# A two-layer SSM-convolution and GeGLU kernel: the last down add of a visit, ahead of or behind the next feature tile's gelu and product

## The chip, the cores and the metric

The kernel runs on one core of a Trainium2 chip. The metric is the device time of one execution in microseconds (us); lower is better. The engines are named as the profile names them: PE (TensorE, matmuls; PEld is its weight loads), DVE (VectorE), ACT (ScalarE), POOL (GpSimd) and SP (SyncE, which here issues DMAs). Each engine runs its own list of instructions in order and waits on semaphores for the others.

## The reference

Two layers of the same pair of steps over a sequence of 2048 positions with 576 channels, batch 1. Step A is a gated long convolution, step B a GeGLU feed-forward with 4608 features. Both normalise their input.

```python
def _A_ref(q, k, v, shift_k, ssm_k, ssm_D):
    ...                       # k_shift: causal filter of 4 taps over k
    kv = k_shift * v
    ...                       # y: causal convolution of kv with ssm_k (2048 taps a channel) by FFT
    y = y + kv * ssm_D[None, None, :]
    return q * y

def _B_ref(x, w_gate, w_up, w_down):
    return (_gelu(x @ w_gate) * (x @ w_up)) @ w_down

x = A_q
x = x + _A_ref(_layernorm(x, axis=-1), A_k, A_v, A_shift_k, A_ssm_k, A_ssm_D)
x = x + _B_ref(_layernorm(x, axis=-1), B_w_gate, B_w_up, B_w_down)
x = x + _A_ref(_layernorm(x, axis=-1), A_k, A_v, A_shift_k, A_ssm_k, A_ssm_D)
x = x + _B_ref(_layernorm(x, axis=-1), B_w_gate, B_w_up, B_w_down)
return x
```

Inputs, weights and output are bf16. The convolution part depends on k, v and the filters alone, so both layers share its result; only the gate q differs.

## The kernel before

The sequence is cut into four chunks of 512 rows (`CH`), and a chunk into four row quarters of 128 (`RT`, index `j`). A *unit* is one layer of one chunk; there are eight. The convolution is done chunk by chunk by a blocked transform made of small matmuls (`cps` tiles, lines 288 and 331) with products and sums on DVE.

The feed-forward sets the frame. Its 4608 features are 36 tiles of 128, in three phases of 12 (`FP`). The units are taken in passes, `[[0], [1, 2], [3, 4], [5, 6], [7]]`; within a pass, each phase is done for each of its units, so that a weight tile serves two units. One phase of one unit is a *visit* (the loop at line 1354); there are 24, counted from 0. A visit has two parts:

- Twelve feature tiles (line 1387). For each, `gu` (line 889) issues 18 matmuls that make gate and up, 128 features by 512 rows each, in one PSUM tile; then ACT makes `ga` = gelu(gate) and DVE makes `hT` = `ga` times up (lines 1410 and 1411; in the early visits, while `hurry()` holds, lines 1401 to 1403 copy `up` out by ACT as well).
- Four row quarters (`j`). For each, 24 down matmuls (line 1426) make `dn`, 128 rows by 576 channels, in a PSUM tile, and DVE adds it to the running `x_c`.

The add has several forms. In the first phase it is line 1466 (it also takes off a mean that an earlier step left in), in the second line 1468, in the third line 1460 for layer 0 (it also sums the row, for the next normalisation). These three are made by `plus` and put into the queue `late` with the planner's time at which the matmuls will be done. In layer 1's third phase the add (line 1447) writes the output tile and is issued at once, without `late`.

PSUM has four such tiles. One is the convolution's (`cps`); the other three are handed out in turn by `pr`, to `gu`, `dn` and, between downs, to further `cps`. A tile is free for its next matmuls once whatever reads it is done: `hT` for a `gu`, the add for a `dn`. `pr` counts what it hands out in `taken` and puts out a late add at the latest when its tile is about to come round again.

The order of instructions on every engine is fixed while the program is built. There is no scheduler behind it (`manual_schedule`); a small clock model, `Pace`, keeps an estimated time for PE (`t.pe`), DVE and ACT, and greedy steps use it. `fill(limit, ...)` (line 941) is called after every feature tile and after every down step. It issues due loads, then late adds (`run_late`, line 624: the first in the queue if its time has come and DVE would be done by `limit`), then convolution steps and normalisation steps for DVE as far as they fit, then ACT steps, then convolution matmuls. Weight loads (`load_wgu`, `load_wd`) and the transposes that make a unit's `xnT` (`spread`, line 841) all go out on SP's queue; rows that are late are turned on PE instead (`turn_row`, line 897).

For a feature tile the order of recording is: `gu`, then gelu and `hT`, then `fill`. At the first tile of a visit the add of the previous visit's fourth row quarter is as a rule still in `late`, since the last down step is not followed by a `fill`. `run_late` reads

```python
if not late or late[0][0] > t.pe or max(t.dve, t.pe - 1.0) + C_EVD > limit:
    return False
```

and `NEVER` is 1e9.

Of the kernel before, what the change touches and what calls it, by code (L numbers as in the profile page):

```python
# [27 lines left out]
NEVER = 1e9  # L28
# [553 lines left out]
def ssm_geglu_kernel(ctx, tc, A_q, A_k, A_v, A_shift_k, A_ssm_k, A_ssm_D, B_x, B_w_gate, B_w_up,  # L582
# [41 lines left out]
    def run_late(limit):  # L624
        if not late or late[0][0] > t.pe or max(t.dve, t.pe - 1.0) + C_EVD > limit:
            return False
        ready, _, run = late.popleft()
        run()
        t.on_dve(C_EVD, ready)
        return True  # L630

    def pr(name):
        while late and taken[0] - late[0][1] >= 2:
            ready, _, run = late.popleft()
            run()
            t.on_dve(C_EVD, ready)
        taken[0] += 1
        return bank(turn[(taken[0] - 1) % 3], name)
# [247 lines left out]
    def gu(pair, w, gi, cols, xnT):  # L886
        for k in range(NKC):
            for s, r0 in ((0, 0), (1, HK)):
                nc.tensor.matmul(cols(pair[:, s, :]), lhsT=w[r0:r0 + HK, k, gi * P:(gi + 1) * P],  # L889
                                 rhs=cols(xnT[r0:r0 + HK, blk_of[k], :]), start=(k == 0), stop=(k == NKC - 1))  # L890

    def gu_half(pair, fi, n):
        gu(pair, wgu[fi // FG], fi % FG, lambda a: a.rearrange("p (j q) -> p j q", q=P)[:, n::2, :], xnT_of[0])
# [27 lines left out]
    def when_due(when, load, n):  # L921
        due.append((when, len(due), load, n))
        due.sort(key=lambda d: d[0])
# [17 lines left out]
    def fill(limit, tensor, conv_first):  # L941
        weights()
        conv.run_loads()
        spreads(tensor=tensor)
        while True:
            if run_late(limit):
                continue
            if conv_first:
                if not (conv.run_v(limit) or run_vq(limit)):
                    break  # L950
            elif not (run_vq(limit) or not pressing() and conv.run_v(limit)):
                break
        run_aq(min(limit, t.pe + 2.3))
        if tensor:
            for _ in range(3):
                if pressing() and (units[coming[0]][1], RT - 1) in conv.y_at or not conv.run_p():
                    break
# [10 lines left out]
    with tc.manual_schedule():  # L968
# [385 lines left out]
        for at, (wb, ph, ui, first, final) in enumerate(visits):  # L1354
# [32 lines left out]
            for fi in range(FP):  # L1387
                n, gi = divmod(wb * FP + fi, FG)
                w = wgu[n]
                if wb == 0 and fi in early:  # L1390
                    pair = early.pop(fi)
                    taken[0] += 1
                    gu_half(pair, fi, 1)
                    t.pe = max(t.pe, free.popleft()) + C_GU / 2
                else:
                    pair = pr("gu")
                    gu(pair, w, gi, lambda a: a, xnT)
                    t.pe = max(t.pe, free.popleft()) + C_GU
                if hurry() and t.act <= t.pe + 0.2:
                    ga = work.tile([P, 2, CH], BF16, tag="ga", name="ga")  # L1400
                    nc.scalar.activation(out=ga[:, 0, :], in_=pair[:, 0, :], func=ACT.Gelu_apprx_tanh)  # L1401
                    nc.scalar.copy(out=ga[:, 1, :], in_=pair[:, 1, :])  # L1402
                    nc.vector.tensor_tensor(out=hT[:, fi, :], in0=ga[:, 0, :], in1=ga[:, 1, :], op=ALU.mult)  # L1403
                    there = t.on_act(2 * C_GELU, max(t.pe + 0.15, gone[0]))
                    gone.append(t.on_dve(C_HB, there + 0.15) + 0.1)
                    free.append(there + 0.1)
                    lead = FAR
                else:
                    ga = work.tile([P, CH], F32, tag="ga", name="ga")
                    nc.scalar.activation(out=ga[:], in_=pair[:, 0, :], func=ACT.Gelu_apprx_tanh)  # L1410
                    nc.vector.tensor_tensor(out=hT[:, fi, :], in0=ga[:], in1=pair[:, 1, :], op=ALU.mult)  # L1411
                    gone.append(t.on_dve(C_HT, t.on_act(C_GELU, max(t.pe + 0.15, gone[0])) + 0.15) + 0.1)
                    free.append(gone[-1])
                    lead = LEAD
                if gi == FG - 1 and final:
                    when_due(t.pe + (FP - FG) * C_GU + 12.0, load_wgu, n + 3)
                fill(t.pe + C_GU + lead, hurry(), conv.left > 0)
# [57 lines left out]
@with_exitstack  # L1475
def kernel(
    ctx: ExitStack,
    tc: tile.TileContext,
    A_q: bass.AP,
    A_k: bass.AP,  # L1480
    A_v: bass.AP,
    A_shift_k: bass.AP,
    A_ssm_k: bass.AP,
    A_ssm_D: bass.AP,
    B_x: bass.AP,
    B_w_gate: bass.AP,
    B_w_up: bass.AP,
    B_w_down: bass.AP,
    out: bass.AP,
):  # L1490
    ssm_geglu_kernel(tc, A_q, A_k, A_v, A_shift_k, A_ssm_k, A_ssm_D, B_x, B_w_gate, B_w_up,
                     B_w_down, out)
# [30 lines left out]
```

## Time and profile before

| | us |
|---|---|
| median of 3 runs | 954.97 (954.17 to 955.44) |
| profiled execution, its own time | 954.88 |
| profiled execution, span from the first to the last instruction | 953.1 |
| granted PE clock, mean (1 is full) | 1.000 |

Where the profile's page groups instructions by line, the rows that the change is about are these:

| line, engine, what | count | mean ns |
|---|---|---|
| L889 PE `gu` matmul, 512 columns | 5130 | 376 |
| L1426 PE `dn` matmul, 288 columns | 2304 | 286 |
| L1410 ACT gelu | 256 | 597 |
| L1411 DVE `hT` | 256 | 686 |
| L1466 DVE add, first phase | 28 (and 4 of the first unit) | 815 |
| L1468 DVE add, second phase | 32 | 751 |
| L1460 DVE add, third phase of layer 0 | 16 | 755 |
| L1447 DVE add to the output tile | 15 | 753 |

Busy times of pipelined matmuls overlap, so 376 ns is not the distance between two of them: ten tiles of 18 `gu` matmuls take 19.60 us in the chain of waits, 1.96 a tile. Ends of matmuls are modelled; starts are recorded.

How to read it: the page gives busy shares of the engines and the chain of work that ended last. A wait is named with the engine and line that ended it. "Stretches" are windows in time, with the busy time of each engine in them.

### The profile page before, as it was taken

To read this page: it belongs to the slowest core of one execution; us is meant where nothing else is said; L and a number is where in the kernel's file an instruction comes from. 1 tells how busy PE (TensorE), PEld (TensorE's weight loads), DVE (VectorE), ACT (ScalarE), POOL (GpSimd) and SP (SyncE) were. 2 spreads that over 40 slices of the span, in tenths; PEclk is the share of its full clock that TensorE was granted. 3 is DMA by queue.
4 is the path that set the end of the run, shared out by engine and by line. 5 is a ranking of instruction groups with operands and counts; after the bars stand their busy time and mean duration, and the time that the engine had idled before them with its cause. 6 is when DMAs were issued, how large, how long until landed. Compare 5 with 4: busy or idle time off the path is not lost.

```text
span 953.1 us, 19333 instructions
## 1 busy us (share of the span) xinstructions
PE 933.3 (98%) x8225; PEld 536.5 (56%) x8225; DVE 550.0 (58%) x1034; ACT 326.2 (34%) x590; POOL 136.2 (14%) x302
## 2 busy tenths in 40 slices
PE   8899999999999999999999999999999999999998
PEld 5756456564655655556556556456456456456455
DVE  7776676586898866667887722553332333532322
ACT  5665426442324136441222511551211214411211
POOL 3214101221113004221110200130000002100000
PEclk9999999999999999999999999999999999999999
DMA  9998997348724803993771730591540540596630
GB/s 238 268 238 203 271 250 145 113 87 224 224 76 132 198 1 88 175 250 86 160 226 38 139 85 22 93 204 33 110 115 1 114 111 8 96 245 151 144 68 26
DMA packets 125323, 130.14 MB, mean 137 GB/s; under 512 B 39730, under 2 KB 117427, under 8 KB 125236
## 3 DMA queue, kind: packets, MB, share of 16 engines
q1 hardware_dynamic: 115906, 92.46, 45.3%
q0 software_dynamic: 9200, 35.54, 12.1%
q8 instruction: 64, 1.05, 0.5%
q10 hardware_dynamic: 130, 0.90, 0.3%
q14 instruction: 23, 0.19, 0.1%
HBM read 108.53 MB, written 11.80 MB: 126 GB/s over the span
## 4 chain that ended last, share of the span: by engine, by line
PE 87%; DVE 5%; DMA 5%; ACT 2%; issue 1%; SPq 0%; ACTq 0%; DVEq 0%
PE gu L889 55%; PE dn L1426 28%; DMA nat<-in_A_ssm_k_dram 2%; PE cps L288 2%; DVE hT L1411 1%; ACT ga L1410 1%; PE cps L331 1%; DMA wgu<-in_B_w_gate_dram 1%; DVE x_c L1466 1%; DMA Hd<-hh 1%; PE ps L889 1%; DMA k<-in_A_k_dram 1%; DVE x_c L1468 1%; PE ps L1092 0%; DVE x_c L1460 0%
## 5 line engine op out<-in xcount | busy, mean ns | idle before, releaser
L889 PE MATMUL gu<-xnT,wgu 64*128 64x512 bf16 x5130 | 562.1, 376 | 4.8 <-DVE x_c L1466 1.8
L889 PEld LDWEIGHTS <-wgu 64*128 64x128 bf16 x5238 | 251.8, 94 | 315.3 <-issue 8.2
L1411 DVE TENSOR_TENSOR hT<-ga,gu 128x512 bf16<-128x512 f32 x256 | 175.7, 686 | 252.8 <-ACT ga L1410 251.5
L1410 ACT ACTIVATE ga<-gu 128x512 f32<-128x512 f32 x256 | 152.8, 597 | 491.1 <-PE gu L889 485.1
L1426 PE MATMUL dn<-wd,hT 128*128 128x288 bf16 x2304 | 294.3, 286 | 0.5 <-DVE xn L1436 0.5
L1426 PEld LDWEIGHTS <-hT 128*128 128x128 bf16 x2304 | 223.5, 98 | 66.0 <-issue 10.5
L721 POOL TENSOR_SCALAR means<-s 128x1 f32<-128x1 f32 x28 | 11.2, 401 | 267.7 <-DVE x_c L1460 224.8
L1468 DVE TENSOR_TENSOR x_c<-x_c,dn 128x576 f32<-128x576 f32 x32 | 24.0, 751 | 32.3 <-PE dn L1426 32.3
L291 ACT ACTIVATE eo<-cps 128x576 f32<-128x576 f32 x48 | 30.9, 651 | 26.9 <-PE cps L288 14.9
L737 POOL TENSOR_TENSOR rstd<-ve,neghalf_t 128x1 f32<-128x1 f32 x56 | 34.4, 615 | 4.7
L308 DVE TENSOR_TENSOR prod<-prod 128x576 bf16<-128x576 bf16 x72 | 33.0, 458 | 2.5
L1466 DVE SCALAR_TENSOR_TENSOR x_c<-dn,means,x_c 128x576 f32<-128x576 f32 x28 | 22.8, 815 | 19.8 <-PE dn L1426 19.7
L1401 ACT ACTIVATE ga<-gu 128x512 bf16<-128x512 f32 x29 | 17.3, 597 | 44.5 <-PE gu L889 41.2
L397 POOL DMA_DIRECT2D kr<-Kd x24 | 13.1, 546 | 100.5 <-DVE prod L307 100.5
L401 POOL DMA_DIRECT2D hr<-Hd x36 | 19.4, 541 | 45.4 <-DVE prod L307 45.4
L1403 DVE TENSOR_TENSOR hT<-ga 128x512 bf16<-128x512 bf16 x31 | 13.0, 421 | 20.8 <-ACT ga L1402 20.8
L1447 DVE TENSOR_TENSOR xn<-x_c,dn 128x576 bf16<-128x576 f32 x15 | 11.3, 753 | 23.0 <-PE dn L1426 23.0
L729 ACT ACTIVATE junk<-x_c,nm 128x576 bf16<-128x576 f32 x28 | 21.5, 767 | 4.9 <-POOL nm L721 4.9
L1460 DVE SCALAR_TENSOR_TENSOR x_c<-dn,x_c 128x576 f32<-128x576 f32 x16 | 12.1, 755 | 18.1 <-PE dn L1426 17.8
L763 ACT ACTIVATE yh<-y,rstd 128x576 f32<-128x576 bf16 x28 | 21.4, 767 | 3.1 <-POOL rstd L737 2.3
L721 POOL TENSOR_SCALAR nm<-s 128x1 f32<-128x1 f32 x28 | 8.6, 308 | 90.0 <-DVE x_c L773 89.9
L296 DVE TENSOR_TENSOR kc<-eo 128x288 bf16<-128x288 f32 x48 | 19.3, 453 | 3.7 <-ACT eo L291 2.2
(148 smaller groups left out, 601.5 us busy)
## 6 DMA issues: line engine op xcount, KB each, us to landing
wgu<-in_B_w_gate_dram SPq DMA_DIRECT2D x45, 576.0 KB, 6.0
wd<-in_B_w_down_dram SPq DMA_DIRECT2D x30, 864.0 KB, 8.9
wgu<-in_B_w_up_dram SPq DMA_DIRECT2D x45, 512.0 KB, 8.0
hr<-Hd POOLq DMA_DIRECT2D x36, 288.0 KB, 6.1
kr<-Kd POOLq DMA_DIRECT2D x24, 288.0 KB, 5.9
Kd<-kc POOLq DMA_DIRECT2D x12, 288.0 KB, 3.8
Hd<-hh POOLq DMA_DIRECT2D x12, 288.0 KB, 3.9
k<-in_A_k_dram POOLq DMA_DIRECT2D x3, 1008.0 KB, 11.6
```

Of the source, the lines that this page charges most:

```text
L291: nc.scalar.activation(out=eo[:], in_=ps[:, :, 0:HW], func=ACT.Copy, scale=scale)
L308: nc.vector.tensor_tensor(out=dst, in0=pr[:, 0, :], in1=pr[:, 1, :], op=ALU.subtract if part == 0 else ALU.add)
L721: nc.gpsimd.tensor_scalar(out=v["nm"][:], in0=v["s"][:], scalar1=-1.0 / D, scalar2=None, op0=ALU.mult)
L729: nc.scalar.activation(out=junk[:], in_=get_x(), func=ACT.Square, bias=v["nm"][:, 0:1], accum_out=v["ss"][:])
L737: nc.gpsimd.tensor_tensor(out=v["rstd"][:], in0=ve[:], in1=neghalf_t[:, 0:1], op=ALU.pow)
L763: nc.scalar.activation(out=g["yh"][:], in_=conv.y[c][:, j, :], func=ACT.Identity, scale=g["rstd"][:, 0:1], bias=1.0)
L889: nc.tensor.matmul(cols(pair[:, s, :]), lhsT=w[r0:r0 + HK, k, gi * P:(gi + 1) * P], rhs=cols(xnT[r0:r0 + HK, blk_of[k], :]), start=(k == 0 ...
L1410: nc.scalar.activation(out=ga[:], in_=pair[:, 0, :], func=ACT.Gelu_apprx_tanh)
L1411: nc.vector.tensor_tensor(out=hT[:, fi, :], in0=ga[:], in1=pair[:, 1, :], op=ALU.mult)
L1426: nc.tensor.matmul(acc[:, h, 0:HW], lhsT=hT[:, fi, j * P:(j + 1) * P], rhs=wd[2 * wb + fi // WT][:, fi % WT, h * HW:(h + 1) * HW], start=( ...
L1466: nc.vector.scalar_tensor_tensor(out=xh, in0=acc[:, :, 0:HW], scalar=m_[:, 0:1], in1=xh, op0=op, op1=ALU.add)
L1468: nc.vector.tensor_tensor(out=xh, in0=xh, in1=acc[:, :, 0:HW], op=ALU.add)
```

## The change

Two lines are added in the loop over feature tiles, behind `gu` and ahead of the tile's gelu and product. They call `run_late` with no limit until the first add in the queue is not yet ready by the planner's clock or none is left.

```diff
                     pair = pr("gu")
                     gu(pair, w, gi, lambda a: a, xnT)
                     t.pe = max(t.pe, free.popleft()) + C_GU
+                while run_late(NEVER):
+                    pass
                 if hurry() and t.act <= t.pe + 0.2:
                     ga = work.tile([P, 2, CH], BF16, tag="ga", name="ga")
```

Lines below the place have numbers higher by two in the changed kernel: the adds of lines 1460, 1466 and 1468 become 1462, 1468 and 1470, the output add of 1447 becomes 1449, and `hT` of 1411 becomes 1413.

## The prediction

> **What bounds the kernel now.** I read the page's busy shares first, then the chain, then who waited for whom on the weight-load queue, then the stretches visit by visit, then one boundary instruction by instruction. A visit is one pass of the loop over `visits`: 12 feature tiles of gate/up matmuls (`gu`, 18 each) and then four row quarters of down matmuls (`dn`, 24 each). I count visits from 0; there are 24.
>
> The page:
>
> ```profile
> span 953.1 us, 19333 instructions
> PE 933.3 (98%) x8225; PEld 536.5 (56%) x8225; DVE 550.0 (58%) x1034; ACT 326.2 (34%) x590; POOL 136.2 (14%) x302
> ...
> PE 87%; DVE 5%; DMA 5%; ACT 2%; issue 1%; SPq 0%; ACTq 0%; DVEq 0%
> ```
>
> TensorE (PE) sets the end: 87% of the chain. The 5% of VectorE (DVE) and 2% of ScalarE (ACT) are places where PE stands still. The waits of PE's weight loads (waiter, releaser: us in total, times, longest) say where:
>
> ```profile
> PEld L889 <- DVE x_c L1466: 5.8, 8, 0.9
> PEld L889 <- DVE x_c L1468: 5.2, 8, 0.8
> ...
> PEld L889 <- DVE x_c L1460: 2.8, 4, 0.7
> ```
>
> L889 is `gu`; L1466, L1468 and L1460 are the three forms of the down add. 8 + 8 + 4 = 20 waits. There are 23 boundaries between visits, and three of them follow a visit of layer 1's last phase, whose add is L1447 and never enters `late`. So every boundary behind a late add has one wait, and no other has. One boundary in the chain, piece by piece (start, length, what):
>
> ```profile
> 734.95 0.73 PE dn L1426 x6
> 735.69 2.07 PE gu L889 x18
> ...
> 737.78 0.60 ACT ga L1410
> ...
> 738.40 0.69 DVE hT L1411
> 739.09 0.68 DVE x_c L1468
> ...
> 739.81 1.25 PE gu L889 x9
> ```
>
> The fourth down ends at 735.7, but its add starts at 739.0: it stands on DVE behind `hT` of feature tile 0, which needs gelu, which needs the whole of `gu` 0. The third feature tile takes the PSUM bank that the add reads, so its matmuls start at 739.81 instead of two tiles (2 x 1.96 us) after 735.62, at 739.54. DVE itself was idle for 4.87 us ahead of that `hT`.
>
> What a wait costs is read from the stretches between first `gu` starts (length, PE busy, ...):
>
> ```profile
> 735.62:771.21 35.59, 35.45 (x313) 19.66 (x313) 11.18 (x16) 7.16 (x12) 0.00 (x0) 1.00 0.52 102
> 806.80:842.47 35.67, 35.46 (x313) 19.67 (x313) 14.77 (x28) 11.62 (x22) 6.58 (x16) 1.00 0.69 121
> 842.47:877.75 35.28, 35.28 (x313) 19.74 (x312) 11.46 (x16) 7.16 (x12) 0.54 (x1) 1.00 0.78 182
> ```
>
> Same matmuls, same granted clock of 1.00. The last one follows an L1447 add, which starts at 842.58, right behind its down, and it takes 35.28 us. Behind L1468 a visit takes 35.59, behind L1466 or L1460 35.66 or 35.67. The kernel holds its own experiment: an add that is put out at once costs PE nothing.
>
> **The change part by part.** It adds no instruction. The new loop puts out every add that the planner's clock calls ready, after `gu` of a tile is recorded and before that tile's gelu and `hT`. In the order of the changed program (built, not run), the fourth add stands directly ahead of the next visit's first `hT` at all 20 boundaries, where it stood directly behind it before.
>
> *Removed: 20 waits.* Behind L1466: seven of 35.66 - 35.28 = 0.38, and the first (visit 1 takes 35.87) of 0.60, 3.26 in all. Behind L1468: seven of 0.31; visit 2 carries other work, its idle time there is 0.35 where the 0.31 ones show 0.14 and the 0.38 ones 0.20, so with the same 0.17 to 0.18 on top it is 0.53; 2.70 in all. Behind L1460: four of 0.38 to 0.39, 1.54. Sum 7.50 us. The add costs nothing in its new place: it takes 0.75 to 0.82 us from about 735.7, and the `hT` behind it can't start before gelu ends at 738.38, 1.9 us after the add. In loaded visits up to six convolution steps stand before the add, but there too DVE was idle before `hT` 0 (2.95 us at 135.3). Late next would be tile 3, which needs the bank of `hT` 0: `hT` 0 ends at 739.09, tile 3 is due at 741.5, 2.4 us of cover. Had the `hT`s to slip by the add's 0.75, 1.6 would be left.
>
> The idle column and the stretches differ. PE's waits for the three adds sum to 1.8 + 0.8 + 0.4 = 3.0 us, and seven of 0.14 that are too short for that list make it 4.0, not 7.5. The Trainium skill ("Perfetto Trace Analysis", section "Tensor Engine Instruction (MATMUL, LD_WEIGHTS)") states that a TensorE end time is estimated by the profiler and not observed; by the idle column the gain would be 4.0, by the starts 7.5. I go by the starts, since 35.59 against 35.28 is measured between starts alone.
>
> *Moved: the greedy planner's later choices.* As DVE's clock is charged earlier, visits 2 to 4, 6 to 8 and 12 come out with their matmuls in another order; that of the other 17 is unchanged. One move has a price. In visit 2 the last of the three rows turned on PE stands at the very end, so the next visit waits for its copy (start, length):
>
> ```profile
> 172.84 0.52 PE cps L905 x9
> ...
> 173.38 0.77 DVE xnT L910
> ...
> 174.19 2.13 PE gu L889 x18
> ```
>
> PE idles 0.85 us there, 1.02 between starts by the same 0.17. In the changed order four convolution and four down matmuls stand between, 8 x 0.124 = 0.99 us (a down phase is 11.87 us for 96), against a copy of 0.77 and two hops. I take 0.8 saved; bounds 1.0 saved and, if the row is not ready four down matmuls earlier, 0.5 lost.
>
> *Re-dealt: convolution tiles between downs.* Visits 3, 4, 7 and 8 take 40.10, 40.90, 44.64 and 40.56. Undisturbed they would take 35.28 plus 0.124 for each of 32 (in visit 7, 64) further matmuls: 39.24 and 43.19. Less the add's wait that leaves 0.48, 1.28, 1.14 and 0.93, together 3.8 us of waits for evacuations and crosses. Their new order has the same number of tiles at similar spacing; visit 8 gets exactly the spacing that visit 4 had. I take no change; bounds: all 3.8 gone, or doubled.
>
> *Queues.* SyncE: in visit 8 the third pair of transposes of visit 9's `xnT` now stands behind one weight load (three DMAs) instead of before it. Before, that load was issued at 389.8, the last pair at 396.4, landing by 406.0; the first reader starts at 411.64: 5.6 us of cover, so 0. GpSimd: small statistics and spills change places, and the mean behind L1460 starts some 3 us earlier; no wait of PE hangs on them at the boundaries. DMA issues are the same in number.
>
> *Sum.* 953.1 - 7.5 - 0.8 = 944.8 us of span. The profiled execution took 954.88, 1.8 over its span, and the median shown is 954.97, 0.1 from it. So 946.6.
>
> **The rivals.**
>
> *The adds go, but the re-dealt order gives part back.* For: DVE is 65 to 85% busy in visits 1 to 8, and 3.8 us already wait there. Against: no step is added. If these waits double, 950.4; with the turned row's saving gone too, 951.2. If only the idle column's 4.0 comes back, 946.6 + 3.5 = 950.1.
>
> *The change doesn't do what it says*: tile 2 waits for something else that is as late, say its weights or `hT` 0. Against: the 35.28 visits, and the 0.72 us between `hT` 0's end and tile 2's start, which is the add's length. About 955.
>
> *Slower: visit 9 starves for `xnT`.* One mechanism: two pairs of transposes behind a weight load on SyncE while the DMA engines are 94% busy (371 to 412). The slowest transpose took 13.6 us to land. A delay up to 5.6 us is free; from 5.6 + 8.3 = 13.9 it eats all that is gained. At 20 us it gives 955 + 6 = 961. For: SyncE stood for 44 us at 327 on one such pair with nothing issued behind it, and a load issued at 403 landed at 417. Against: the load waits for no buffer at that point (its group's last reader, visit 8's first four tiles, is done by 379), so it goes out before 389.8 rather than after, and the pair behind it loses at most the load's 6.5 us of issue.
>
> **How the numbers follow.** The forecast, 944 to 949, has 0.64. The part given back (949 to 953) has 0.18, no effect (within 0.2%, 953.1 to 956.9, what a measurement of this kernel can't tell from no change) 0.05, slower 0.08, and all waits of the convolution gone as well (below 943.5, down to 946.6 - 3.8 - 0.2 = 942.6) 0.05. Faster: 0.64 + 0.18 + 0.05 = 0.87. Range 943.5 to 951.2, the upper end being the doubled waits without the turned row: 0.64 and most of 0.18, about 0.8.
>
> **What would show it.** Right: L1466, L1468 and L1460 gone from the waits of L889; visits behind them 35.28 long; the add starting within 0.2 us of its down's end in the last third; PE's share of the chain up and DVE's near 2 to 3%. The turned row: no 0.85 us of idle at the start of visit 3. Wrong would be: tile 2 still starting late with another releaser; tile 3 waiting for `hT` 0; visits 3, 4, 7, 8 longer than 40 to 45 us by more than they give; or PE waiting for `xnT` at the start of visit 9.

## The result, and the profile after

The changed kernel takes 947.87 us (median of 7 runs, 947.52 to 953.15) against 954.97 before (954.17 to 960.04): ratio 0.9923, 95% interval 0.9897 to 0.9949. The forecast was 946.6, range 943.5 to 951.2. The profiled execution has a span of 946.1, against 953.1 before and 944.8 in the forecast's sum. Some executions of either kernel take 4 to 6 us longer than the rest, which widens these ranges.

The page of the changed kernel, busy shares and chain:

```profile
span 946.1 us, 19330 instructions
PE 930.2 (98%) x8225; PEld 539.2 (57%) x8225; DVE 552.5 (58%) x1033; ACT 327.5 (35%) x591; POOL 137.5 (15%) x302
...
PE 96%; DVE 2%; DMA 1%; ACT 1%; issue 0%; POOL 0%; SPq 0%; ACTq 0%; DVEq 0%
```

Busy times hardly move: nothing became cheaper. DVE's part of the chain falls from 5% to 2%, and PE's rises from 87% to 96%. (Part of that rise is in the first 90 us, where the chain runs through DMAs before and through PE now, although visit 1 starts at 96.2 in both.)

Who PE waited for, in the changed kernel (us in total, times, longest):

```profile
PE cps L288 <- DVE x_c L1468: 2.0, 3, 0.7
PE cps L288 <- ACT eo L291: 1.3, 3, 0.7
...
PE gu L889 <- DMA xnT<-xn: 0.6, 1, 0.6
PE dn L1428 <- DVE xn L1438: 0.5, 1, 0.5
```

No `gu` (L889) waits for an add any more. One `gu` wait is new: for a DMA that makes `xnT`. The waits of `cps` tiles between downs are still there.

A boundary that answers to the one at 735.6, in the timeline (start, length, engine, line, what, idle time before):

```profile
730.30 4.92 PE L889 MATMUL gu<-xnT,wgu 64*128 64x512 bf16 x44
730.41 0.76 DVE L1470 TENSOR_TENSOR x_c<-x_c,dn 128x576 f32<-128x576 f32 x1 [2.19 <-PE dn L1428]
732.46 0.60 ACT L1412 ACTIVATE ga<-gu 128x512 f32<-128x512 f32 x1 [13.32 <-PE gu L889]
733.09 0.69 DVE L1413 TENSOR_TENSOR hT<-ga,gu 128x512 bf16<-128x512 f32 x1 [1.93 <-ACT ga L1412]
```

The add starts 0.11 us after the visit's first `gu` matmul, instead of 3.4 us after it. `hT` still waits for gelu, 1.93 us after the add has ended, and `gu` runs on without a break. The stretches from first `gu` to first `gu` (length, PE busy, ...), two behind a late add and one behind an output add, then visits 2 and 3:

```profile
553.89:589.17 35.28, 35.28 (x313) 19.76 (x314) 11.28 (x16) 7.16 (x12) 1.70 (x3) 1.00 0.19 63
730.30:765.59 35.29, 35.29 (x314) 19.78 (x314) 11.28 (x16) 7.16 (x12) 0.00 (x0) 1.00 0.52 102
836.15:871.44 35.29, 35.29 (x315) 19.77 (x314) 11.47 (x16) 7.16 (x12) 0.54 (x1) 1.00 0.72 169
131.47:173.16 41.69, 41.69 (x376) 24.47 (x376) 28.76 (x65) 23.02 (x43) 7.14 (x18) 1.00 0.82 175
173.16:214.29 41.13, 39.21 (x341) 24.16 (x341) 26.88 (x55) 19.90 (x38) 12.30 (x30) 1.00 0.49 132
```

The visits 1 to 22 that hold no convolution matmuls are now all 35.28 or 35.29 long. From visit 9 on the saving is 4.2 us, as in the forecast's sum for those visits. The miss is in visits 2 to 8: 2 and 3 together took 82.26 before and take 82.82, although two add waits worth 0.91 left them.

### The profile page after: what moved, and what is told of

Its sections match the earlier page's. It is cut to its first block, busy times and chain, and to the rows that moved or that the text cites. A ratio compares the mean times of both kernels' runs of the same rounds, so it can differ in the third digit from the quotient of the medians.

```text
span 946.1 us, 19330 instructions
## 1 busy us (share of the span) xinstructions
PE 930.2 (98%) x8225; PEld 539.2 (57%) x8225; DVE 552.5 (58%) x1033; ACT 327.5 (35%) x591; POOL 137.5 (15%) x302
## 4 chain that ended last, share of the span: by engine, by line
PE 96%; DVE 2%; DMA 1%; ACT 1%; issue 0%; POOL 0%; SPq 0%; ACTq 0%; DVEq 0%
PE gu L889 59%; PE dn L1428 29%; PE cps L288 2%; PE ps L279 2%; PE cps L331 1%; PE ps L889 1%; DMA k<-in_A_k_dram 1%; PE ps L1092 1%; PE ps L1198 1%; PE ps L1124 0%; PE ps L1219 0%; DVE x_c L1468 0%; DMA xnT<-xn 0%; DVE kc L296 0%; DVE x_c L1462 0%
## 5 line engine op out<-in xcount | busy, mean ns | idle before, releaser
L889 PE MATMUL gu<-xnT,wgu 64*128 64x512 bf16 x5130 | 559.0, 377 | 0.6 <-DMA xnT<-xn 0.6
L889 PEld LDWEIGHTS <-wgu 64*128 64x128 bf16 x5238 | 254.9, 94 | 304.7 <-issue 8.5
L736 POOL TENSOR_SCALAR ve<-ss 128x1 f32<-128x1 f32 x56 | 14.9, 266 | 39.3 <-ACT junk L729 39.2
```

## The experiments

Three kinds: the place of the add apart from the planner's re-dealing, the price of the add where it stands, and the last stretch of idle time at the end.

**Place alone.** The add's instruction is split from its bookkeeping. The instruction goes out early, the planner's clock is charged where it was before, so that every other instruction on every engine keeps its order.

```diff
+                for q in late:
+                    if q[0] <= t.pe:
+                        q[3]()
                 if hurry() and t.act <= t.pe + 0.2:
...
-                    late.append((t.pe + 0.2, taken[0], plus))
+                    late.append((t.pe + 0.2, taken[0], plus, op))
```

> The kernel before, with its planner's clock and every later choice kept; only the 20 fourth adds stand ahead of the next visit's first hT (20 pairs swapped on VectorE, every other instruction of every engine in the old order). Theory (the place of the add alone removes the waits): the 20 waits of 7.5 us are gone, the 0.85 us of idle time for the turned row at the start of visit 3 and the waits between downs in visits 3, 4, 7 and 8 stay as before: span 945.6, time about 947.4, a little below the changed kernel's 947.87. Rival (the gain came from the re-dealt order): about 955.

Measured: 947.57 us, ratio 0.9914 (0.9896 to 0.9932), span 945.8. The page's row for `gu`, before and here (busy, mean ns, then PE's idle time ahead of it and what ended most of that):

```profile
L889 PE MATMUL gu<-xnT,wgu 64*128 64x512 bf16 x5130 | 562.1, 376 | 4.8 <-DVE x_c L1466 1.8
...
L889 PE MATMUL gu<-xnT,wgu 64*128 64x512 bf16 x5130 | 558.7, 376 | 0.8 <-DVE xnT L910 0.8
```

The 20 waits are gone; the 0.85 us for the turned row at the start of visit 3 and the waits in visits 3, 4, 7 and 8 stay. The place of the add is the whole gain: 7.3 us of span, and 7.46 from the start of visit 1 to the end, against 7.50 in the sum. The re-dealt order is worth a little less than nothing: 946.1 with it, 945.8 without. The medians can't tell these two apart, but the visits can: in two traces of the changed kernel no visit from 1 to 22 differs by more than 0.01 us.

**The planner's new order, with late adds.** The reverse split: the clock and all later choices as in the changed kernel, the 20 instructions behind `hT` 0.

```diff
+                held_ops[0] = []
+                while run_late(NEVER):
+                    pass
+                kept, held_ops[0] = held_ops[0], None
                 if hurry() and t.act <= t.pe + 0.2:
...
+                for op in kept:
+                    op()
                 if gi == FG - 1 and final:
```

> The changed kernel's planner clock and all its later choices, but the 20 fourth adds stand behind the first hT again. Theory: the 20 waits come back on the new order, 947.9 + 7.5 = 955.4; against the kernel before this shows the price of the re-dealt order alone, 0.5 us by my reading of the two traces. Rival (the new order is the gain): near 948.

Measured: 964.96 us, ratio 1.0092 (1.0065 to 1.0118), well above both the theory and the rival. Three things are in it. First, 18 waits are back at their old size, by the lengths of the visits. Second, two are far larger. The chain at the start of visit 7 (start, length, what):

```profile
340.09 2.07 PE gu L890 x18
...
343.50 0.68 DVE x_c L1478
...
344.22 4.11 PE gu L890 x23
```

Here only 18 `gu` matmuls run before PE stands, not 36. In the new order a `cps` tile was handed out after the fourth down's, so tile 1 and not tile 2 takes the add's bank, and PE idles 2.08 us (at visit 3, 2.15). In the changed kernel these two adds are early and cost nothing. Third, the profiled execution reached visit 1 7.3 us later than the kernel before. DVE, and PE behind it, wait there for a store of `Hd`: it starts 1.7 us later and takes 9.25 us to land instead of 6.47. PE stands for 3.67 us, and then needs 2.8 us more for the way to visit 1, at a granted clock of 0.50 to 0.57 from 94 to 100 us. All of this lies ahead of the first moved add. It varies from run to run: with one pass added to the kernel before (below), which leaves this stage as it is, the store took 8.62 us. Why it varies is not settled. The executions of the kernel with late adds have spans from 959.1 to 966.4. So its time can't price the new order, and it was run again with those two adds early:

```diff
+                if at in (3, 7):
+                    for op in kept:
+                        op()
+                    kept = []
```

> As the kernel with the new order and late adds, but with the adds ahead of hT 0 at the starts of visits 3 and 7, where in the new order tile 1 and not tile 2 takes the add's bank. Theory (18 of the 20 waits are back, and the new order alone costs about what the place-only kernel shows against the changed one, 0.3 us of span): 946.1 + 7.50 - 0.38 - 0.31 = 952.9 of span, time 954.7. Rival (the new order itself is dear): 957 or more.

Measured: 955.02 us, ratio 1.0000 (0.9976 to 1.0023), span 953.0. The kernel before less these two waits would be 953.1 - 0.69 = 952.4, so the new order alone costs 0.6 us of span with late adds; with early ones it is 946.1 - 945.8 = 0.3. Counted from the start of visit 1, which leaves out the stage that varies, the two agree: 0.45 and 0.43.

**Part of the boundaries.** The change holds from visit 13 on alone, where no matmul moves.

```diff
-                while run_late(NEVER):
+                while at >= 13 and run_late(NEVER):
                     pass
```

> The change at the nine boundaries from visit 13 on alone; no matmul moves. Theory: the nine waits are worth 4 x 0.31 + 3 x 0.38 + 2 x 0.39 = 3.16 us, so 955.0 - 3.2 = 951.8, span 949.9. Rival (waits are passed on down the line, or some cost hides in the idle column): 953.1 by the idle column, which shows 4 x 0.14 + 5 x 0.20 = 1.6 us for these nine plus nothing else.

Measured: 951.77 us, ratio 0.9964 (0.9948 to 0.9980), span 949.8. The profiled spans differ by 3.3, and from the start of visit 13 to the end by 3.1, so the idle column's 1.6 is refuted by the traces. The interval of the times, 950.2 to 953.3 against 955.16 for the kernel before beside it, would by itself not exclude 953.1. A wait costs the distance between starts, about 0.17 us more than the idle time shown.

**A longer way to the bank.** DVE passes that add zero times the down tile stand in front of the fourth add at the nine boundaries from visit 13 on. One on the kernel before, three and six on the changed one.

```diff
                     def plus(c=c, j=j, ..., at=at):
+                        for _ in range(6 if at >= 12 and j == RT - 1 else 0):
+                            nc.vector.scalar_tensor_tensor(out=xh, in0=acc[:, :, 0:HW], scalar=0.0, in1=xh, op0=ALU.mult, op1=ALU.add)
```

> The kernel before, with one more DVE pass over the down tile (it adds zero times the tile, 0.67 us from start to start as the adds' neighbours show) in front of the fourth add at the nine boundaries from visit 13 on. Theory (tile 2 waits for the end of the add, which is queued behind hT 0): each of the nine waits grows by the pass, 9 x 0.67 = 6.0, time 961.0. Rival (tile 2 waits for something else that ends at the same time): about 955.

> The changed kernel with three such passes in front of the fourth add at the same nine boundaries: the add then ends about 0.1 + 3 x 0.67 + 0.75 = 2.9 us after the visit's start, tile 2 is due at 3.9 and hT 0 can't start before 2.8. Theory (the add's work is covered): no change, 947.9, visits 35.28 long. Rival (DVE work ahead of hT 0 costs what it takes): 9 x 2.0 = 18 us more, 966.

> The changed kernel with six such passes: the add ends 0.1 + 6 x 0.67 + 0.75 = 4.9 us after the visit's start, one microsecond after tile 2 is due. Theory (the point from which it decides is the due time of tile 2): about 0.95 us at each of nine boundaries, 8.5 in all, 956.4; between 954 and 962. Rival (only hT's own chain matters, with 2.4 us of slack for tile 3): hT 0 ends at 5.6 against 5.9, no change.

Measured: one on the kernel before, 962.74 us (ratio 1.0076, 1.0043 to 1.0109); three on the changed one, 948.12 (0.9913, 0.9882 to 0.9945); six, 964.16 (1.0081, 1.0049 to 1.0113). In the first, the nine visits are 36.39 or 36.45 and 36.46 long, 0.79 more each, 7.1 in all against the 6.0 expected. (Its profiled execution was 964.68; it also reached visit 1 2.7 us late, with the store of `Hd` as above.) In the second they are 35.28: 27 DVE passes that cost nothing. In the third they are 37.06 to 37.13, 1.8 more each. The timeline of the third:

```profile
737.97 4.06 PE L889 MATMUL gu<-xnT,wgu 64*128 64x512 bf16 x36
738.08 4.72 DVE L1461 SCALAR_TENSOR_TENSOR x_c<-dn,x_c 128x576 f32<-128x576 f32 x6 [2.19 <-PE dn L1428]
...
742.83 0.75 DVE L1472 TENSOR_TENSOR x_c<-x_c,dn 128x576 f32<-128x576 f32 x1
...
743.64 1.68 PE L889 MATMUL gu<-xnT,wgu 64*128 64x512 bf16 x14 [1.61 <-DVE x_c L1472]
```

Six passes take 4.72 us, 0.79 from one to the next, not the 0.67 that I took from neighbours which don't read what the one before has written. The add ends at 743.6, 5.6 us into the visit, and tile 2, due 3.92 us in, starts as it ends. So 9 x 1.8 = 16 us was measured where 8.5 was expected, and the upper bound of 962 was missed; the point from which the add decides, the due time of tile 2, holds.

**The end.** The last row quarter is done in two halves of 288 columns, and the second half's matmuls waited for the read of the first half.

```diff
                     for h in range(2):
+                        if h:
+                            acc = pr("dn")
                         for fi in range(FP):
```

> The changed kernel with a second PSUM tile for the second half of the very last down, so that its first matmul need not wait for the read of the first half (0.545 us idle at 941.1 in the changed kernel). Theory: 0.545 + 0.17 = 0.7 us less, span 945.4, time 947.2. Rival (the tail behind it, the last add and the store, sets the end anyway): no change.

Measured: 947.01 us, ratio 0.9909 (0.9891 to 0.9927), span 945.6. Up to its last matmul, the last visit shrinks from 36.06 to 35.35, by 0.71, and its wait is gone from the list; 0.2 of it is lost in the span to a later start of visit 1 (96.4 against 96.2).

**Together.** The place-only kernel with the last half's own tile, beside the changed kernel on the same chip.

> The place-only kernel together with the second PSUM tile for the last half. Theory (both gains are where PE stands still and add up): 945.8 - 0.71 = 945.1 of span, 946.9, which is below both kernels. Rival (the two meet in the same wait): 947.6, as the place-only kernel.

> The changed kernel itself on the same chip as the combined one, to set the two side by side: 947.9, one microsecond above the combined kernel if the theory holds.

Measured: 946.70 us (ratio 0.9914, 0.9889 to 0.9940), span 944.9, against 948.08 (0.9930, 0.9908 to 0.9953) for the changed kernel. By the medians it is 1.4 us below the changed kernel beside it; the two intervals overlap. The traces give 1.2 from the start of visit 1 to the end.

## Why the prediction was right

*What bounds the kernel* was right: PE, with 20 waits at visit boundaries that the order on DVE made.

*The 20 waits, 7.50 us.* Shown by the place-only kernel (7.46 from the start of visit 1) and by the nine boundaries alone (3.1 to 3.3 for 3.16). The choice between the idle column and the starts was the one that mattered: 4.0 against 7.5, and the runs take the starts' side. This agrees with the statement of the Trainium skill ("Perfetto Trace Analysis", section "Tensor Engine Instruction (MATMUL, LD_WEIGHTS)") that TensorE ends are estimated. Here about 0.17 us of each wait does not show as idle time.

*The add costs nothing in its new place.* Shown from visit 13 on by three passes more for nothing, and by six that cost only what passes the due time of tile 2. In the loaded visits the place-only kernel shows it: visits 2 to 8 are each shorter by their wait (0.31 to 0.52).

*The turned row, 0.8 saved: wrong in size.* The copy of the third turned row is covered as forecast, but only three of the four rows are turned on PE. The remaining one goes by SP's transposes, and the chain of the changed kernel at the start of visit 3 (start, length, what) ends on it:

```profile
170.94 0.59 DVE xn L802
171.53 0.02 SPq L844
...
171.59 2.52 DMA xnT<-xn
...
174.15 1.88 PE gu L889 x15
```

PE idles 0.60 us there in place of 0.85, so that 0.25 was saved. The transposes of this row were in the trace of before (issued at 169.6 and 170.9, 2.5 us or more to land), but they were not followed, as the copy behind them came later. In the new order they also go out later, 38.8 us into visit 2 instead of 37.6.

*The re-dealt tiles, taken as no change: nearly right in sum, by luck.* Against the place-only kernel, which has the old order, the changed one takes 1.47 more in visits 2 and 3 together, 1.04 less in visit 4, 0.29 less in visits 6 and 7 and 0.28 more in visit 8: 0.4 more in sum, the turned row's 0.25 included. The prediction gave no reason why such parts should cancel. Most of the 1.47 is two waits of `cps` tiles between the downs of visit 3, where the place-only kernel has one of 0.13 (start, length, what, idle time before):

```profile
204.31 0.28 PE L288 MATMUL cps<-ht,T 128*128 128x288 bf16 x1 [0.66 <-ACT eo L291]
...
207.59 0.28 PE L288 MATMUL cps<-ht,T 128*128 128x288 bf16 x1 [0.66 <-DVE x_c L1468]
```

"The same number of tiles" was also misread: about half of visit 7's 64 further matmuls moved to visit 6, which takes 39.20 instead of 35.28, while visit 7 takes 40.13 instead of 44.34.

*The miss.* From the start of visit 1 the forecast saved 8.3 us and 7.03 were measured. Of the 1.27 between them, 0.55 is the turned row, 0.68 the re-dealt tiles and 0.04 the 20 waits.

*Queues, 0.* Visit 9 is 35.29 long and starts without a wait for `xnT`; the weight load that moved ahead of two transposes did no harm.

*The rivals.* "Gives part back" came true by about a microsecond, inside the forecast's own band. "Doesn't do what it says" and "visit 9 starves" fell by the waits that are gone and by visit 9's start.

## What to carry to other kernels

An instruction that frees a buffer and whose input is long ready should stand ahead of one that must still wait, on an engine that works through its list in order: here DVE sat idle for 4.87 us behind `hT` while a finished add kept PE from its bank. Price such a wait by the distance between starts of otherwise equal stretches, not by the idle time shown, and look for a stretch that is free of it already, as the visits behind the output add were. When a planner's clock is touched, test the edit once with the old order kept; and check which tile comes round to a buffer first, since two of the new order's boundaries needed it one tile sooner.

## What was not expected of the hardware

A short stop of PE can cost more than its length. In the kernel with the new order and late adds, PE idled 2.08 us before 344.2, and the granted clock then fell for about 5 us (stretch, ..., granted clock third from the end):

```profile
345.00:347.00 2.00, 2.00 (x16) 0.81 (x12) 0.62 (x1) 0.00 (x0) 0.00 (x0) 0.62 0.00 0
347.00:350.00 3.00, 3.00 (x22) 1.10 (x18) 2.12 (x3) 0.60 (x1) 0.00 (x0) 0.69 0.00 0
350.00:352.00 2.00, 2.00 (x22) 0.92 (x20) 1.36 (x2) 0.65 (x2) 0.00 (x0) 1.00 0.04 8
```

That visit took 44.07 us, 3.94 more than the changed kernel's 40.13, of which the stop explains 2.08 + 0.17 and the lower clock the rest (0.38 of 2 us and 0.31 of 3 us are 1.7). A stop of 2.15 us at 186.6 in the same execution left the clock at 1.00, and one of 3.67 at 93.9 brought it down to 0.50. A stop of 3.05 at 92.1 in the run with one pass on the kernel before, and nine of 1.60 to 1.67 in the run with six passes, left it at 1.00 too. So the length of a stop alone does not decide; what does was not tried.

DVE passes over the same tile in a row, each reading what the one before has written, follow each other at 0.79 us, against 0.67 between adds and unrelated neighbours. Products and the sums that read them (lines 304 and 308) stand 0.78 to 0.79 apart in the kernel before as well. That the reading is the cause was not tested by itself.
